# A fused attention and gated-MLP block: second pair of rows turned by products, value rows of the first block ahead of the second block, sums, scales and splits one product apart, first maxima in twos

## The chip, the cores and the metric

One core of one Trainium2 chip runs the whole program. The metric is device time in microseconds, smaller is better; the time given for a kernel is the median of its runs. A profile is one further execution, recorded by the hardware profiler. Engines: PE is TensorE (matrix products), DVE is VectorE, ACT is ScalarE, POOL is GpSimd, SP is SyncE, which here only issues DMAs. PEld is PE's loading of weights.

## The reference

The input `x` has 2048 rows of 576 numbers. A layer norm, an attention of 32 heads of 18 numbers each, a second layer norm and a gated MLP of width 4608 follow, each half with its residual:

```python
qkv = (x @ wqkv).reshape(B, S, 3, H, Dh)            # x: layer norm of A_x
scores = jnp.einsum("bhqd,bhkd->bhqk", q, k) * Dh ** -0.5
p = _softmax(scores, axis=-1)
o = jnp.einsum("bhqk,bhkd->bhqd", p, v)
h = x + o @ wo
...
g = jnp.einsum("bsd,df->bsf", x, w_gate)            # x: layer norm of h
u = jnp.einsum("bsd,df->bsf", x, w_up)
h2 = h + jnp.einsum("bsf,fd->bsd", _gelu(g) * u, w_down)
```

Only the first part matters here: layer norm, the product with `wqkv`, and the start of the attention.

## The kernel before

**Numbers in two halves.** A float32 operand is cut into a rounded float16 part ("high") and the float16 of what is left ("low"). A product of two such operands is three float16 products, high by high, low by high and high by low. Weights are multiplied by a power of two before they are cut: `norm_w` sums their squares on ACT (five passes, L155), adds them over the partitions with one small product on PE (L158) and makes the scale from the result in seven short DVE steps. `split_cols` then makes the high part on ACT (L283) and the low part on DVE (L284). `cut(s, j)` does so for the 128 columns of query and key tile `j`; the value weights (`wf[2]`) are cut in two halves of 288 columns, and land in the memory that `wf[0]` leaves.

**Rows.** The 2048 rows are 16 row tiles of 128, four to a block; there are four blocks. For a row tile, `row_stats` takes mean and variance on DVE (L188, L189), `rstd_of` the reciprocal root for a group of row tiles (root on ACT, the rest on DVE), `normed` the normalized row in place (DVE, L236), `split_rows` the high part on ACT (L248) and the low part on POOL or DVE (L249, L250), and `turn` the transposed row tile, by a transposing DMA (L253) into `XT`, which holds all rows with the 576 features on the partitions. Features 0 to 511 are chunks 0 to 3 (high) and 5 to 8 (low); chunk 4 holds the last 64, high and low. `rstd_beside` is `rstd_of` done by 12 short POOL steps; before, only a later part of the program used it.

**Products of this stage.** `qk_tile(j, b)` makes 128 columns of queries or keys for the 512 rows of block `b`: 14 products of 512 columns (L300) in one of four PSUM banks (`m_ring` over `singles`), then the high part by ACT (L352), the low part by DVE (L353), and two DMAs to DRAM (L355, L356). `v_rows(t)` makes the values of a row tile: twice 14 products of 288 columns in one of two pairs of banks, evicted by ACT (L368, L370). A generator yields after half of the products and after the rest; `take(it, n)` runs `n` such steps.

**Order.** PE, ACT, DVE and POOL run each in the order in which the code is written (`in_order`). So does SP inside its own `manual_schedule`, which before ended with `v_rows(3)`; behind it the framework places SP's DMAs. The order written is: rows 0 and 1 (norm, split, turn), 9 idle products, rows 2 and 3 with 18 idle products (`idle_products`: products that nothing reads), query and key tiles of block 0 with the cutting of their weights and the norms of rows 4 to 11 between them, first tiles of block 1, `v_rows(0)` to `v_rows(3)`, and the other tiles 0, 4 and 5 of blocks 1 to 3.

**Start of the attention.** `init_set(sets[0])` writes constant rows by four DMAs and `load_stacks(0)` loads queries and keys of four heads back from DRAM, one pair of heads by 12 DMAs of SP and one by 12 of POOL. The softmax needs a maximum for each row; `maxima()` makes each from a product (L589) in a bank of `m_ring` and a DVE reduction of 0.68 us (L601). Its steps make 2, 1, 2, 1 and 2 products, in this order. Before the attention's own loop, 60 such steps (L1183) run in turns with 72 steps of `other_products()` (the other values and tiles, "fill"), after 14 steps of fill alone.

Of the kernel before, what the change touches and what calls it, by code (L numbers as in the profile page):

```python
# [18 lines left out]
P = 128  # L19
D = 576  # L20
# [3 lines left out]
NK = 4  # L24
# [7 lines left out]
def tile_block(  # L32
# [202 lines left out]
    def normed(dst, src, t):  # L235
        nc.vector.tensor_scalar(dst, src, rs[:, t : t + 1], nb[:, t : t + 1],  # L236
                                op0=ALU.mult, op1=ALU.add)
# [9 lines left out]
    def split_rows(dst, src, copy=nc.scalar.copy, sub=nc.vector.tensor_sub):  # L247
        copy(dst[:, :D], src)  # L248
        sub(dst[:, LM:], src[:, : NK * P], dst[:, : NK * P])  # L249
        sub(dst[:, D:LM], src[:, NK * P :], dst[:, NK * P : D])  # L250

    def turn(rows, t):
        nc.sync.dma_start_transpose(XT[:, :, t * P : (t + 1) * P], rows)  # L253
# [3 lines left out]
    def load_w(dst, src, eng):  # L257
        eng.dma_start(dst[:, :NK, :], src[: NK * P, :].rearrange("(c p) n -> p c n", p=P))
# [22 lines left out]
    def split_cols(wf, sc, wh, wl):  # L281

        nc.scalar.activation(wh, wf, AF.Copy, scale=sc)  # L283
        nc.vector.scalar_tensor_tensor(wl, wf, sc, wh, op0=ALU.mult, op1=ALU.subtract)  # L284
# [17 lines left out]
    def run(it):  # L302
        for _ in it:
            pass

    def result(it):
        while True:
            try:
                next(it)
            except StopIteration as end:  # L310
                return end.value

    def take(it, n=1):
        for _ in range(n):
            next(it, None)
# [27 lines left out]
    def load_x(b):  # L343
        nc.sync.dma_start(nat[:, b * TPB : (b + 1) * TPB], xv[:, b * TPB : (b + 1) * TPB])

    def qk_tile(j, b, bank):
        sl = slice(b * TB, (b + 1) * TB)
        hl = next(tmp3_ring).bitcast(F16).rearrange("p (a b) -> p a b", a=2)
        hi, lo = hl[:, 0], hl[:, 1]
        yield from accumulate(bank[:, :TB], [(w, a) for a, w in products(  # L350
            sl, *wqk[j], slice(0, P))])
        nc.scalar.activation(hi, bank[:, :TB], AF.Copy, scale=2.0 ** -16)  # L352
        nc.vector.scalar_tensor_tensor(lo, bank[:, :TB], 2.0 ** -16, hi,  # L353
                                       op0=ALU.mult, op1=ALU.subtract)
        nc.sync.dma_start(qk_hi[j * P : (j + 1) * P, sl], hi)  # L355
        nc.sync.dma_start(qk_lo[j * P : (j + 1) * P, sl], lo)  # L356
        yield
# [19 lines left out]
    def norm_w(i):  # L377

        e = yield from norm_exponent(wf[i], f"w{i}")
        e_w.append(e)  # L380
        return pow2(e, -1, 268, f"s_w{i}")

    def cut(s, *js):

        for j in js:
            for i in range(2):
                a, b = max(j * P, i * D), min((j + 1) * P, (i + 1) * D)
                if a < b and s[i] is not None:
                    h, l = (w[:, :, a - j * P : b - j * P] for w in wqk[j])
                    split_cols(wf[i][:, :, a - i * D : b - i * D], s[i], h, l)  # L390
# [3 lines left out]
    def ln_stats(t0, n):  # L394
        for t in range(t0, t0 + n):
            row_stats(nat[:, t], t)

    def ln_rows(t0, n, **engines):
        for t in range(t0, t0 + n):
            normed(nat[:, t], nat[:, t], t)  # L400
        for t in range(t0, t0 + n):
# [19 lines left out]
    def idle_products(n):  # L421

        for _ in range(n):
            nc.tensor.matmul(pairs2[0][:, 0], id16, parts[0][:, :512], start=True, stop=True)

    with tc.manual_schedule(engines={EngineType.SP}):
        n0, n1, n2 = norm_w(0), norm_w(1), norm_w(2)
        s = [None, None]
        ln_stats(0, 2)
        rstd_of(0, 2, root=True)  # L430
        ln_rows(0, 2, **on_pool)
        load_chunks(wf[1], wqkv[:, D:QK], nc.sync, (0, 1))
        idle_products(9)
        ln_stats(2, 2)
        take(n0, 2)
        rstd_of(2, 2, root=True)
        for t in (2, 3):
            normed(nat[:, t], nat[:, t], t)
        take(n0, 3)
        split_rows(parts[2], nat[:, 2], **on_pool)  # L440
        s[0] = result(n0)
# [5 lines left out]
        load_chunks(wf[1], wqkv[:, D:QK], nc.sync, range(2, NK + 1))  # L447
        load_x(1)
        qk_tiles(0, 0)
        take(n1, 4)  # L450
        qk_tiles(0, 1)
        load_x(2)
        take(n1, 1)
        it = qk_tile(2, 0, next(m_ring))
        next(it)
        s = [None, result(n1)]
        cut(s, 4)
        run(it)
        cut(s, 5)
        ln_stats(4, 2)  # L460
        qk_tiles(0, 3)
        cut(s, 6, 7, 8)
        ln_stats(6, 2)
        rstd_of(4, 4, root=True)
        qk_tiles(0, 4)
        ln_rows(4, 2, **on_pool)
        load_w(wf[2], wqkv[:, QK:], nc.sync)
        qk_tiles(0, 5)
        ln_rows(6, 2, **on_pool)
        ln_stats(8, 2)  # L470
        qk_tiles(0, 6)
        load_x(3)
        ln_stats(10, 2)
        rstd_of(8, 4, root=True)
        take(n2, 3)
        qk_tiles(0, 7)
        take(n2, 2)
        ln_rows(8, 2, **on_pool)
        qk_tiles(0, 8)
        ln_rows(10, 2, **on_pool)  # L480
        it = qk_tile(0, 1, next(m_ring))
        next(it)
        s_v = result(n2)
        run(it)
        split_cols(wf[2][:, :, :HALF], s_v, *wv[0])
        ln_stats(12, 2)
        qk_tiles(1, 4)
        split_cols(wf[2][:, :, HALF:], s_v, *wv[1])
        ln_stats(14, 2)
        rstd_of(12, 4, root=True)  # L490
        qk_tiles(1, 5)
        ln_rows(12, 2, **on_pool)
        run(v_rows(0))
        run(v_rows(1))
        ln_rows(14, 2, **on_pool)
        run(v_rows(2))
        run(v_rows(3))
    qk_tiles(2, 0, 4, 5)
    qk_tiles(3, 0, 4, 5)
    nc.vector.tensor_add(e_w[0], e_w[0], e_w[1])  # L500
# [842 lines left out]
```

## Time and profile before

| | us |
|---|---|
| median of 3 runs | 2673.91 (2672.24 to 2674.68) |
| profiled execution, time | 2668.08 |
| profiled execution, span | 2666.3 |
| PE busy | 2589.7 (97%) |
| DVE busy | 2013.1 (76%) |
| ACT busy | 1619.2 (61%) |
| POOL busy | 777.3 (29%) |

A timeline gives for each merged piece its start, its length, the engine, the line, the operation with output and inputs, the count, and in brackets the idle time of the engine ahead of it and what ended that. A windows view gives busy time (and instructions) of each engine in a stretch, the clock granted to PE, the DMA engines' busy share and GB/s. A groups view gives busy time and mean ns of one instruction. The profiled execution was 5.8 us shorter than the median of the runs; differences are worked out inside it and then taken from the median.

### The profile page before, as it was taken

Reading aid. Unit: us, or ns where it says so; the run is one execution under the profiler, and the core shown is the slowest. Engines: PE = TensorE matmul, PEld = TensorE weight load, DVE = VectorE, ACT = ScalarE, POOL = GpSimd, SP = SyncE. Lnnn points to the kernel's source line nnn. Section 1 sums busy time; section 2 is a strip of 40 time slices with the busy share of each in tenths; the row PEclk is TensorE's granted clock in tenths of the full one; section 3 lists DMA queues with packets and bytes.
Section 4 is the critical chain, followed back from the end, with each engine's and each line's share of the span. In section 5 each row is a group of like instructions: output and inputs, shape, how many; then the busy total and the mean of one; then the engine's idle time right before and its main releaser. Section 6 shows DMA issues by size and latency. Waiting matters only on the chain.

```text
span 2666.3 us, 44517 instructions
## 1 busy us (share of the span) xinstructions
PE 2589.7 (97%) x16665; PEld 1118.6 (42%) x16665; DVE 2013.1 (76%) x3872; ACT 1619.2 (61%) x2128; POOL 777.3 (29%) x1040
## 2 busy tenths in 40 slices
PE   6999999999999999999999899999999999999999
PEld 2542222222222222222243555555555555555555
DVE  6367999999999999999967866566666666666653
ACT  5215999999999999999956433333333333333332
POOL 2200352132223232221666532222222222222221
PEclk9999999999999999999999999999999999999999
DMA  8411101010101010110116321010101010101010
GB/s 222 94 40 51 54 26 30 19 42 15 42 14 45 17 42 19 30 25 20 36 47 125 74 51 40 23 40 23 40 22 40 24 39 25 38 27 36 29 59 36
DMA packets 171466, 114.70 MB, mean 43 GB/s; under 512 B 90872, under 2 KB 149772, under 8 KB 171250
## 3 DMA queue, kind: packets, MB, share of 16 engines
q1 hardware_dynamic: 163566, 99.06, 13.9%
q0 software_dynamic: 7552, 12.79, 1.8%
q8 instruction: 130, 2.13, 0.3%
q14 instruction: 86, 0.70, 0.1%
q10 hardware_dynamic: 132, 0.01, 0.0%
HBM read 76.51 MB, written 15.01 MB: 34 GB/s over the span
## 4 chain that ended last, share of the span: by engine, by line
PE 67%; ACT 15%; issue 7%; DVE 4%; POOL 2%; DMA 2%; SPq 0%; ACTq 0%; DVEq 0%; POOLq 0%
PE more L1065 14%; PE bank L1065 13%; ACT WK L644 10%; PE bank L300 10%; PE bank L648 9%; PE more L300 8%; PE bank L589 7%; PE pair L300 4%; ACT nat L595 4%; PE pair L642 2%; DVE mx L601 1%; DMA nat<-rc 1%; ACT nat L662 0%; POOL A L996 0%; DMA V<-V 0%
## 5 line engine op out<-in xcount | busy, mean ns | idle before, releaser
L644 ACT ACTIVATE WK<-pair 128x1024 f32<-128x1024 f32 x1024 | 1000.0, 1041 | 84.8 <-PE pair L642 84.1
L601 DVE TENSOR_REDUCE mx<-bank 128x1 f32<-128x512 f32 x1552 | 975.7, 683 | 42.8 <-PE bank L589 32.4
L648 PE MATMUL bank<-WK,V 128*32 128x512 f32 x4096 | 547.7, 606 | 0.2 <-ACT nat L662 0.2
L300 PEld LDWEIGHTS <-WK 128*128 128x128 f16 x3456 | 338.0, 98 | 90.9 <-ACT WK L1076 1.7
L1065 PEld LDWEIGHTS <-W 128*128 128x128 f16 x2394 | 234.3, 98 | 282.9 <-issue 5.7
L589 PE MATMUL bank<-W 54*128 54x512 f16 x896 | 258.2, 379 | 14.0 <-DVE mx L601 1.8
L589 PE MATMUL bank<-A 54*128 54x512 f16 x904 | 255.0, 380 | 16.8 <-DVE mx L601 5.3
L671 POOL TENSOR_TENSOR rp<-rc,minus_one 128x16 f32<-128x16 f32 x28 | 81.9, 2926 | 537.1 <-DMA rc<-nat 537.1
L300 PE MATMUL more<-W,WK 128*128 128x288 f16 x1728 | 235.6, 286 | 2.2 <-ACT WK L1076 1.4
L300 PE MATMUL bank<-W,WK 128*128 128x288 f16 x1728 | 235.2, 286 | 0.0
L1065 PE MATMUL bank<-X,W 128*128 128x512 f16 x792 | 223.8, 379 | 0.0
L642 PE MATMUL pair<-A 56*128 56x512 f16 x1024 | 212.9, 381 | 2.3 <-ACT WK L644 1.4
L642 PE MATMUL pair<-W 56*128 56x512 f16 x1024 | 210.3, 380 | 4.3 <-ACT WK L644 3.2
L1065 PE MATMUL bank<-V,W 128*128 128x512 f16 x720 | 202.4, 379 | 0.4 <-ACT tmp L1115 0.3
L936 POOL TENSOR_TENSOR A<-A 128x384 f32<-128x384 f32 x136 | 137.0, 1028 | 202.6 <-DMA A<-in_B_w_up_dram 118.7
L589 PEld LDWEIGHTS <-W 54*128 54x128 f16 x1024 | 75.1, 93 | 283.6 <-issue 266.6
L599 DVE CUSTOM_DVE_ANT_0 nat<-bank,nat 128x512 f32<-128x512 f32 x248 | 171.4, 691 | 27.1 <-PE pair L642 4.4
L589 PEld LDWEIGHTS <-A 54*128 54x128 f16 x1024 | 72.3, 93 | 267.9 <-issue 250.8
L1079 POOL TENSOR_TENSOR WK<-tmp,WK 128x512 f16<-128x512 f32 x73 | 87.9, 1203 | 305.9 <-ACT WK L1076 305.6
L1083 ACT COPY tmp<-more 128x512 f32<-128x512 f32 x36 | 21.0, 583 | 236.8 <-PE more L1065 198.2
L595 ACT ACTIVATE nat<-bank 128x512 f32<-128x512 f32 x248 | 151.4, 611 | 11.5 <-PE bank L589 11.5
L648 PEld LDWEIGHTS bank<-WK,V 128*32 128x32 f32 x4096 | 81.1, 108 | 179.0 <-issue 164.2
(304 smaller groups left out, 3259.9 us busy)
## 6 DMA issues: line engine op xcount, KB each, us to landing
A<-in_B_w_down_dram SPq DMA_DIRECT2D x8, 1152.0 KB
nat<-rc SPq DMA_DIRECT2D x32, 256.0 KB
A<-in_B_w_gate_dram SPq DMA_DIRECT2D x64, 128.0 KB
A<-in_B_w_up_dram SPq DMA_DIRECT2D x64, 128.0 KB
qk_hi<-tmp SPq DMA_DIRECT2D x36, 128.0 KB
qk_lo<-tmp SPq DMA_DIRECT2D x36, 128.0 KB
out_dram<-nat SPq DMA_DIRECT2D x16, 288.0 KB
X<-nat SPq DMA_DIRECT2D x100, 36.0 KB
```

The source lines that it names most:

```text
L300: nc.tensor.matmul(dst, a, b, start=(i == 0), stop=(i == len(pairs) - 1))
L589: nc.tensor.matmul(pm[:, :TB], Q[r, q0 : q0 + P], keys, start=True, stop=True)
L595: nc.scalar.activation(row, pm[:, :TB], AF.Relu)
L599: nc.vector.tensor_tensor_reduce(row, pm[:, :TB], row, 1.0, LOWEST, ALU.add, ALU.max, dst)
L601: nc.vector.tensor_reduce(dst, pm[:, :TB], axis=AX.X, op=ALU.max)
L642: nc.tensor.matmul(pS[:, j, :TB], K[r, kt * P : (kt + 1) * P], Q[r, qc * TB : (qc + 1) * TB], start=True, stop=True)
L644: nc.scalar.activation(pes[(2 * kt + pr) % NPE], pS[:, :, :TB], AF.Exp, scale=ex_reg)
L648: nc.tensor.matmul(acc[32 * hh : 32 * hh + 32, :TB], Vg[n // NB][:, kt * G4 + hh * VC : kt * G4 + hh * VC + 32], pes[(2 * kt + hh // 2) % ...
L671: nc.gpsimd.tensor_tensor(rc, den, minus_one.to_broadcast([P, R]), op=ALU.pow)
L936: op(W8[:, d], W8[:, a], W8[:, b])
L1065: nc.tensor.matmul(bank, w, x_, start=start and i == 0, stop=i == len(mm) - 1, skip_group_check=not start)
L1079: nc.gpsimd.tensor_sub(hl[:, 2 * i + j], v, hh[:, 2 * i + j])
```

## The change

`ln_rows` is cut in two, `ln_norm` and `ln_split`. Row tiles 2 and 3 are no longer turned by DMA: the new `turned` multiplies their chunks by a unit matrix on PE (18 products of 128 columns in five banks) and copies the results to `XT` by three ACT and two DVE instructions; the idle products ahead of it go from 18 to 4. The value weights are loaded behind tile 0 of block 0, ahead of the rows of block 2, and cut during tiles 6 and 7; `v_rows(0)` to `v_rows(3)` stand ahead of all tiles of block 1. Rows 4 to 15 take their scales from POOL (`rstd_beside`), and statistics, scales, norms and splits are spread, one or two between two tiles. SP's own written order goes on until `key_steps(0)` (DMAs of the constant rows, the stacks, the keys' steps). The 60 steps of maxima are taken two at a time (30 turns) with 2 or 3 of fill, in place of 2 or 3 at a time (24 turns) with 3.

```diff
+    def turned(t0):
+
+        cols = slice(t0 * P, (t0 + 2) * P)
+        pts = [pairs2[0][:, 1], pairs2[1][:, 0], next(m_ring), next(m_ring)]
+        for pt, c0 in zip(pts, (0, 2, NK + 1, NK + 3)):
+            for c in range(2):
+                for t in range(2):
+                    o = (2 * c + t) * P
+                    nc.tensor.matmul(pt[:, o : o + P], parts[t0 + t][:, (c0 + c) * P : (c0 + c + 1) * P],
+                                     id16, start=True, stop=True)
+            copy = nc.scalar.copy if c0 < NK else nc.vector.tensor_copy
+            copy(XT[:, c0 : c0 + 2, cols], pt.rearrange("p (c t) -> p c t", c=2))
...
-        idle_products(18)
-        split_rows(parts[3], nat[:, 3])
-        turn(parts[2], 2)
-        turn(parts[3], 3)
-        cut(s, 0, 1, 2, 3, 4)
+    idle_products(4)
+    split_rows(parts[3], nat[:, 3])
+    cut(s, 0)
+    turned(2)
+    cut(s, 1, 2, 3, 4)
     load_chunks(wf[1], wqkv[:, D:QK], nc.sync, range(2, NK + 1))
     load_x(1)
     qk_tiles(0, 0)
+    load_w(wf[2], wqkv[:, QK:], nc.sync)
...
+    take(n2, 2)
+    qk_tiles(0, 4)
+    load_x(2)
+    cut(s, 7)
+    ln_stats(6, 1)
+    take(n2, 3)
+    qk_tiles(0, 5)
+    cut(s, 8)
+    ln_stats(7, 1)
+    rstd_beside(4, 4, 1024.0)
+    it = qk_tile(6, 0, next(m_ring))
+    next(it)
+    s_v = result(n2)
+    run(it)
+    ln_norm(4, 2)
+    split_cols(wf[2][:, :, :HALF], s_v, *wv[0])
+    qk_tiles(0, 7)
+    load_x(3)
+    ln_split(4, 1, **on_pool)
+    split_cols(wf[2][:, :, HALF:], s_v, *wv[1])
+    ln_split(5, 1, **on_pool)
+    ln_norm(6, 2)
+    qk_tiles(0, 8)
+    ln_split(6, 2, **on_pool)
+    ln_stats(8, 3)
+    run(v_rows(0))
+    ln_stats(11, 1)
+    rstd_beside(8, 4, 1024.0)
+    ln_norm(8, 2)
+    run(v_rows(1))
+    ln_split(8, 2, **on_pool)
+    ln_norm(10, 2)
+    ln_stats(12, 2)
+    run(v_rows(2))
+    ln_split(10, 2, **on_pool)
+    ln_stats(14, 2)
+    rstd_beside(12, 4, 1024.0)
+    run(v_rows(3))
+    ln_norm(12, 2)
+    qk_tiles(1, 0)
...
     key_steps(0)
+    sp_order.close()
...
-    for i in range(AHEAD):
-        take(mxs, 2 + i % 2)
-        take(fill, 3)
+    for i in range(5 * AHEAD // 4):
+        take(mxs, 2)
+        take(fill, 2 + (i % 5 in (1, 3)))
```

Three places show how the rows stand on an engine. DVE from the low part of row 3 (L249, L250) to the first eviction, first before and then in the change (`bank`, `pair`: PSUM; `W`: cut weights; `X`: the turned rows):

```order
L249 TENSOR_TENSOR A<-nat,A 128x512
L250 TENSOR_TENSOR A<-nat,A 128x64
L284 SCALAR_TENSOR_TENSOR W<-WK,p_s_w_206,W 128x640 x4
L284 SCALAR_TENSOR_TENSOR W<-WK,p_s_w_206,W 128x5x64
L353 SCALAR_TENSOR_TENSOR tmp_81<-bank_67,tmp_81 128x512
```

```order
L249 TENSOR_TENSOR A<-nat,A 128x512
L250 TENSOR_TENSOR A<-nat,A 128x64
L284 SCALAR_TENSOR_TENSOR W<-WK,p_s_w_206,W 128x640
L439 CAST X<-bank_67 128x2x256
L439 CAST X<-bank_68 128x2x256
L284 SCALAR_TENSOR_TENSOR W<-WK,p_s_w_206,W 128x640 x3
L284 SCALAR_TENSOR_TENSOR W<-WK,p_s_w_206,W 128x5x64
L353 SCALAR_TENSOR_TENSOR tmp_81<-bank_66,tmp_81 128x512
```

Two copies of turned low parts now stand between the low weights of tile 0 and those of tiles 1 to 4.

ACT from the second half of the value weights (L283, 128x1440) to the first evictions of values (L368, L370), before and in the change:

```order
L283 ACTIVATE W<-WK,p_s_w_556 128x1440
L199 ACTIVATE ln_r<-mv,eps 128x4
L352 ACTIVATE tmp_81<-bank_68 128x512
L248 CAST A<-nat 128x576 x2
L368 ACTIVATE V<-pair_73 128x4x4x18
L368 ACTIVATE V<-pair_74 128x3x4x18
```

```order
L283 ACTIVATE W<-WK,p_s_w_447 128x1440
L248 CAST A<-nat 128x576
L352 ACTIVATE tmp_81<-bank_68 128x512
L248 CAST A<-nat 128x576 x2
L368 ACTIVATE V<-pair_73 128x4x4x18
L368 ACTIVATE V<-pair_74 128x3x4x18
L370 ACTIVATE V<-pair_74 128x4x18
L368 ACTIVATE V<-pair_73 128x4x4x18
L368 ACTIVATE V<-pair_74 128x3x4x18
L370 ACTIVATE V<-pair_74 128x4x18
L248 CAST A<-nat 128x576 x2
L368 ACTIVATE V<-pair_73 128x4x4x18
```

The root on ACT (L199) is gone; the high parts of rows 6 and 7 now stand ahead of the evictions of `v_rows(0)`, and those of rows 8 and 9 ahead of the evictions of `v_rows(2)`.

SP around the last stores of this stage (L355, L356), the constant rows (`neg`) and the stacks of the first heads, before and in the change:

```order
L355 DMA qk_hi<-tmp_81 128x512
L356 DMA qk_lo<-tmp_81 128x512
L540 DMA A<-qk_hi 18x2048
L355 DMA qk_hi<-tmp_81 128x512
L356 DMA qk_lo<-tmp_81 128x512
L540 DMA A<-qk_hi 18x2048
L355 DMA qk_hi<-tmp_81 128x512
L541 DMA A<-qk_hi 18x2048
L356 DMA qk_lo<-tmp_81 128x512
```

```order
L355 DMA qk_hi<-tmp_81 128x512
L356 DMA qk_lo<-tmp_81 128x512
L556 DMA A<-neg 2x8x256 x4
L572 DMA A<-qk_hi 18x2048
L573 DMA A<-qk_hi 18x2048
L572 DMA A<-qk_hi 18x2048
L573 DMA A<-qk_lo 18x2048
```

Before, three stack loads were issued ahead of the last store and the constant rows long before; now all four and all twelve stand behind it.

More of the change, by code (lines that the diff above doesn't have):

```diff
@@ L424, in idle_products @@
             nc.tensor.matmul(pairs2[0][:, 0], id16, parts[0][:, :512], start=True, stop=True)
[L426 to L441, printed above, removed]
-        idle_products(18)
-        split_rows(parts[3], nat[:, 3])
-        turn(parts[2], 2)
-        turn(parts[3], 3)
-        cut(s, 0, 1, 2, 3, 4)
[L447 to L497, printed above, removed]
@@ new lines, in turned @@
+    def turned(t0):
[9 more added lines that the diff above has]
+            copy(XT[:, c0 : c0 + 2, cols], pt.rearrange("p (c t) -> p c t", c=2))
+        pt = next(m_ring)
+        for t in range(2):
+            nc.tensor.matmul(pt[:, t * P : (t + 1) * P], parts[t0 + t][:, NK * P : (NK + 1) * P],
+                             id16, start=True, stop=True)
+        nc.scalar.copy(XT[:, NK, cols], pt[:, : 2 * P])
@@ new lines, in tile_block @@
+    sp_order = ExitStack()
+    sp_order.enter_context(tc.manual_schedule(engines={EngineType.SP}))
+    n0, n1, n2 = norm_w(0), norm_w(1), norm_w(2)
+    s = [None, None]
+    ln_stats(0, 2)
+    rstd_of(0, 2, root=True)
+    ln_norm(0, 2)
+    ln_split(0, 2, **on_pool)
+    load_chunks(wf[1], wqkv[:, D:QK], nc.sync, (0, 1))
+    idle_products(9)
+    ln_stats(2, 2)
+    take(n0, 2)
+    rstd_of(2, 2, root=True)
+    ln_norm(2, 2)
+    take(n0, 3)
+    split_rows(parts[2], nat[:, 2], **on_pool)
@@ new lines, in tile_block @@
+    s[0] = result(n0)
+    idle_products(4)
[3 more added lines that the diff above has]
+    cut(s, 1, 2, 3, 4)
+    load_chunks(wf[1], wqkv[:, D:QK], nc.sync, range(2, NK + 1))
+    load_x(1)
+    qk_tiles(0, 0)
+    load_w(wf[2], wqkv[:, QK:], nc.sync)
+    take(n1, 4)
+    qk_tiles(0, 1)
+    take(n1, 1)
+    it = qk_tile(2, 0, next(m_ring))
+    next(it)
+    s = [None, result(n1)]
+    cut(s, 4)
+    run(it)
+    cut(s, 5)
+    ln_stats(4, 1)
+    qk_tiles(0, 3)
+    cut(s, 6)
@@ L498, in tile_block @@
+    ln_split(14, 2, **on_pool)
+    qk_tiles(1, 5)
     qk_tiles(2, 0, 4, 5)
```

9 lines of the change are left out of this document (8 added, 1 removed).

## Prediction

> **What bounds the kernel now.** First the busy time by stage (start, length, then busy us and instructions of PE, PEld, DVE, ACT, POOL; granted clock; DMA share; GB/s): up to the first maxima, the maxima beside fill, the rest.
>
> ```profile
> 0.00:118.60 118.60, 92.43 (x495) 49.80 (x495) 58.22 (x154) 48.26 (x104) 32.27 (x64) 0.96 0.68 174
> 118.60:230.60 112.00, 106.51 (x588) 50.01 (x588) 68.69 (x114) 20.45 (x49) 3.84 (x9) 1.00 0.16 51
> 230.60:2666.30 2435.70, 2390.72 (x15584) 1018.77 (x15583) 1886.21 (x3604) 1550.47 (x1976) 741.21 (x967) 1.00 0.14 36
> ```
>
> PE is the bound; all that the change can reach is its idle time in the first two stages, 26.2 and 5.5 us. Behind 230.6 the same rows follow on each engine, so that part should only shift. PE's timeline shows where it stands still:
>
> ```profile
> 13.29 4.04 PE L424 MATMUL pair<-A,id 128*128 128x512 f16 x18
> 20.41 7.71 PE L300 MATMUL bank<-X,W 128*128 128x512 f16 x35 [3.08 <-DMA X<-A]
> 28.33 19.80 PE L300 MATMUL bank<-X,W 128*128 128x512 f16 x91
> 57.41 3.05 PE L300 MATMUL bank<-X,W 128*128 128x512 f16 x7 [9.28 <-DMA X<-A]
> 76.45 12.12 PE L300 MATMUL pair<-W,X 128*128 128x288 f16 x84 [4.32 <-ACT V L368]
> 88.41 18.29 PE L300 MATMUL bank<-X,W 128*128 128x512 f16 x84
> 106.54 12.17 PE L300 MATMUL pair<-W,X 128*128 128x288 f16 x98
> 124.27 0.37 PE L589 MATMUL bank<-A 54*128 54x512 f16 x1 [0.35 <-DVE mx L601]
> ```
>
> The first useful product starts at 20.41 and waits for a turned row; 9.28 us go to the turned rows of block 1, 4.32 us to an eviction of values. The clock falls in the two long gaps but not after the 3.08 us: the 35 products from 20.41 take 0.22 each.
>
> ```profile
> 56.00:60.00 4.00, 2.60 (x7) 0.95 (x8) 2.10 (x4) 3.53 (x9) 1.46 (x3) 0.50 0.96 201
> 76.00:80.00 4.00, 3.55 (x19) 2.40 (x19) 1.08 (x1) 1.18 (x5) 2.62 (x4) 0.66 0.41 76
> ```
>
> In the second stage nearly all idle time is one wait, 14 times, the longest at the start (us, times, longest):
>
> ```profile
> PE bank L589 <- DVE mx L601: 5.5, 14, 0.9
> ```
>
> **Term 1, first tile.** A tile of 14 products takes 3.02 us at full clock (84 in 88.41 to 106.54, 0.216 each), `v_rows` 3.46 (28 at 0.1235, from the 98 at 106.54).
>
> ```profile
> 10.14 2.85 SPq L253 DMA_TRANSPOSE X<-A  x2
> 15.55 2.77 SPq L253 DMA_TRANSPOSE X<-A  x2
> 14.79 3.44 ACT L283 ACTIVATE W<-WK,p_s_w 128x640 f16<-128x640 f32 x5 [0.66 <-DVE p_s_w L173]
> 14.75 0.77 POOL L250 TENSOR_TENSOR A<-nat,A 128x64 f16<-128x64 f32 x1
> 15.28 0.33 DVE L250 TENSOR_TENSOR A<-nat,A 128x64 f16<-128x64 f32 x1
> ```
>
> ```profile
> L188 DVE BATCH_NORM_STATS2 st<-nat 128x6 f32<-128x288 f32 x32 | 12.7, 438 | 2.8 <-DMA nat<-in_A_x_dram 2.8
> L353 DVE SCALAR_TENSOR_TENSOR tmp<-bank,tmp 128x512 f16<-128x512 f32 x18 | 12.3, 684 | 42.0 <-ACT tmp L352 42.0
> L352 ACT ACTIVATE tmp<-bank 128x512 f16<-128x512 f32 x18 | 10.6, 590 | 22.1 <-PE bank L300 19.5 <-issue 2.6
> L236 DVE TENSOR_SCALAR nat<-nat,rs,nb 128x576 f32<-128x576 f32 x16 | 10.6, 707 | 0.1
> L155 ACT ACTIVATE A<-WK 128x576 f16<-128x576 f32 x15 | 10.1, 672 | 3.5 <-DMA WK<-in_A_wqkv_dram 3.4
> L248 ACT CAST A<-nat 128x576 f16<-128x576 f32 x16 | 9.9, 670 | 8.8 <-DVE nat L236 7.1 <-issue 1.7
> L284 DVE SCALAR_TENSOR_TENSOR W<-WK,p_s_w,W 128x640 f16<-128x640 f32 x8 | 6.6, 880 | 0.1
> L284 DVE SCALAR_TENSOR_TENSOR W<-WK,p_s_w,W 128x1440 f16<-128x1440 f32 x2 | 3.4, 1714 | 0.7 <-ACT W L283 0.7
> ```
>
> Rows 2 and 3 are cut by 15.6 as before. A turning product of 128 columns isn't in the trace; it lies between nothing and 0.22 (the 18 unit-matrix products of 512 columns, 4.04 us). I take 0.11, about its weight load (0.1), so 18 end at 16.5. A copy of 512 columns I take like an eviction: 0.59 on ACT, 0.68 on DVE. ACT makes W of tile 0 from 14.8 to 15.6, then the copies to 17.2; DVE the low W to 16.5, then its two copies to 17.8. The second product needs the first DVE copy, so PE runs from 17.2. Rows 0 and 1 still go by DMA, issued 5.4 us ahead of rows 2 and 3 (used at 20.4), so down by about 15. Tile 0 ends at 17.2 + 13 x 0.216 = 20.0, 3.4 us ahead of before (20.41 + 14 x 0.216 = 23.4).
>
> The Trainium skill, "TensorE: Matmul & The Clock Gate", Part 4 on the PE-mode transpose, gives about 275 ns for a 128x128 transpose and says that such work doesn't count as busy for the clock gate. By it the 18 take 5.0 us, and 1.5 us more go if tile 0 then runs at half clock; the sum below would be some 12 instead of 15. The trace speaks against the second half: 3.08 us of nothing cost no clock.
>
> **Term 2, block 0 and its values.** Tiles 0 to 8, two norm products and four `v_rows` end, without other waits, at 20.0 + 8 x 3.02 + 0.9 + 13.8 = 59.0; a norm product took 0.36 (20.41 to 28.33 less 35 x 0.216), and I give the two 0.9, as ACT's squares come later against PE now. The waits come from in-order chains:
>
> ```profile
> 20.00:40.00 20.00, 19.59 (x92) 8.90 (x93) 11.65 (x31) 9.61 (x21) 0.00 (x0) 1.00 0.72 228
> 46.85 0.64 SPq L258 DMA_DIRECT2D WK<-in_A_wqkv_dram  x1
> 53.92 0.68 ACT L155 ACTIVATE A<-WK 128x576 f16<-128x576 f32 x1 [3.42 <-DMA WK<-in_A_wqkv_dram]
> 50.12 5.08 SPq L253 DMA_TRANSPOSE X<-A  x2
> ```
>
> From 13.0 on (the first turning DMAs are out) the DMAs must bring key weights, block 1, value weights (1.33 + 1.18 + 1.33 MB) and take three tiles' stores (0.8 MB): at 228 GB/s they are done at 33.3; bounds are 29 (issue near 22 plus the 7.1 us of 46.85 to 53.92) and 38. ACT, which squares them (L155) between the evictions, then delays the second norm product by 0.9.
>
> ```profile
> 1395.21 0.23 POOL L225 TENSOR_SCALAR ln_v<-mv 128x2 f32<-128x2 f32 x1 [1.43 <-DVE mv L189]
> 1398.81 0.24 POOL L233 TENSOR_SCALAR nb<-ln_u 128x2 f32<-128x2 f32 x1
> 1405.66 0.31 POOL L225 TENSOR_SCALAR ln_v<-mv 128x2 f32<-128x2 f32 x1
> 1411.93 0.23 POOL L233 TENSOR_SCALAR nb<-ln_u 128x2 f32<-128x2 f32 x1
> ```
>
> The scales on POOL take 3.8 us where DVE lets POOL alone and 6.5 at the other place. I take 4.1: DVE waits for them here and has little else. The squares end at 38.1, so tile 5 is evicted at 38.7 and 39.4, the low weights of tile 8 end at 40.3, the statistics of row 7 at 41.3, the scales at 45.4, the norms of rows 4 and 5 at 46.5, the low value weights at 48.2 and 50.6 (an eviction between), the norms of 6 and 7 at 51.7. PE wants the first low value weights at 46.3: it waits 1.9, then 0.7 for the second half. The eviction of `v_rows(0)` stands behind the casts of rows 6 and 7 (52.4): 0.7. Statistics of rows 8 to 11 end at 56.5, scales at 60.6, the casts of 8 and 9 at 62.4, the eviction behind them at 62.8; PE has wanted that bank since 59.7: 3.1. Values so end at 59.0 + 0.9 + 6.4 = 66.3. Rows 6 and 7 are turned by then: before, the last turned row was down 10.5 us after the load ahead of it (46.85 to 57.41), and that load, block 3, goes out near 49.7, which gives 60.2. That is the cover of the 9.28 us; each microsecond past 66.3 would cost one. The 4.32 us and the slow clock (1.5 us on the 7 products of 57.41, 1.6 on the 84 of 76.45) go too, as no gap passes 3.1 by this sum. Nine tiles end at 66.3 + 27.2 = 93.5, before at 106.5: **13.0 less**.
>
> **Term 3, stacks.**
>
> ```profile
> 71.76 0.86 SPq L524 DMA_DIRECT2D A<-neg  x1
> 108.15 0.33 SPq L356 DMA_DIRECT2D qk_lo<-tmp  x1
> 113.32 0.28 SPq L541 DMA_DIRECT2D A<-qk_hi  x1
> 119.87 0.12 PEld L589 LDWEIGHTS <-A 54*128 54x128 f16 x2 [1.14 <-DMA A<-qk_lo]
> ```
>
> Before, the last of SP's stacks went out 5.2 us behind the last store and was down 6.6 later; PE waited 0.9. Now four constant rows (0.7 to 0.9 each, 2.9) and three more stacks (1.1) lie between: with the store at 94.9 the last goes out at 104.1. Down 6.6 later, it holds PE from 105.9 to 110.7, 3.9 more than before; down 2.1 later (as the turned rows, issued by 18.3, used at 20.4) it costs nothing and the old 0.9 goes. POOL's half still runs beside, but starts earlier: I take **3.0 more**.
>
> **Term 4, maxima in twos.** Turns of 3, 3, 4, 3 and 3 products fit four banks; before, every second turn made 5 and the fifth waited for a reduction.
>
> ```profile
> L601 DVE TENSOR_REDUCE mx<-bank 128x1 f32<-128x512 f32 x1552 | 975.7, 683 | 42.8 <-PE bank L589 32.4
> ```
>
> Three reductions take 2.05 us, a turn with two steps of value fill 0.6 + 1.73: no wait, though thinly; beside tiles (3.02) amply. Of the 5.5 us all but the first 0.9 go: **4.6 less** (bounds 0 and 5.5). Turns and fill are the same in number, so nothing is added.
>
> **Sum.** 13.0 - 3.0 + 4.6 = 14.6. The profiled execution would take 2668.1 - 14.6 = 2653.5; the median, 5.8 above it, 2673.9 - 14.6 = 2659.3.
>
> **Rivals.**
> - *POOL's scales take the longer row.* 2.4 us more, twice, in the chain to the values; the wait of 3.1 becomes 5.5, longer than the 4.32 that lost the clock, so 1.6 more: 2673.9 - 8.2 = 2665.7. For it: both rows are the same twelve steps, and 64 columns of low part took POOL 0.77 at 14.75 beside DVE's 0.33. Against: DVE waits for most of that time. The Trainium skill, "GPSIMD Engine Reference", section 8, says POOL shares its SBUF interfaces with VectorE and contends where that has two SBUF inputs; the longer row would fit, the trace doesn't name its cause. Chance 0.14.
> - *Everything is covered:* no wait among the values (7.3) and none for the stacks: 13.0 + 7.3 + 4.6 + 0.9 = 25.8, 2648. Against it stands the same chain in the 4.32 us of before. 0.10.
> - *The value weights land at 38,* not 33.3: 4.7 us more ahead of the second norm product, 2664. 0.10.
> - *The twos don't do what they say,* since DVE is late for another reason: 4.6 lost, 2663.9. 0.06.
> - *Slower: turned rows of block 1 late.* In SP's order rows 6 and 7 stand behind tile 8's low store, which waits for DVE, and behind block 3's load, with four more turning DMAs next. From 66.3 on each microsecond costs one; the gain is gone when row 7 lands at 80.9, and beyond 86 the kernel is slower by more than 0.2%. A landing at 88 gives 2673.9 + 7.1 + 1.5 (clock) = 2682. For it: the 9.28 us were this very wait. Against: 60.2 by the old rows. 0.05.
>
> **How the numbers follow.** The forecast, 2659, has 0.55. 0.2%, 5.3 us, is about what a measurement of this kernel can tell from no change. Faster by more than that are the forecast but for its edge, and the first four rivals: 0.89; within it 0.07; slower 0.04. The range goes from part of the covered case, 2650, to past the slow scales, 2668; it leaves out the rest of the covered case and the slower one.
>
> **What would show it.** In PE's timeline: first product of a tile near 17 (term 1 wrong if near 20 or at 0.43 a product); value products from about 45 to 66 with waits named L284 and L368; no wait on turned rows; a wait of 3 to 5 us at the first maxima that names the stacks; and no 0.35 us waits behind it. The prediction is wrong if the first maxima start later than about 113, or if PE's busy time behind them grows.

## The result, and the profile after

| | before | after |
|---|---|---|
| median, us | 2672.69 (2667.78 to 2674.68, 6 runs) | 2654.24 (2649.01 to 2655.46, 6 runs) |
| ratio | | 0.9932, 95% interval 0.9922 to 0.9942 |
| profiled execution, time, us | 2668.08 | 2654.51 |
| span, us | 2666.3 | 2652.7 |

The kernel is faster by 18.4 us, with an interval of 15.5 to 20.8 (the ratio's, times 2672.69). The two profiled executions lie only 13.6 us apart; that gap is taken up below. The stages of after, cut at the same three places as before (start, length, then busy us and instructions of PE, PEld, DVE, ACT, POOL; granted clock; DMA share; GB/s):

```profile
0.00:105.30 105.30, 89.93 (x499) 49.12 (x499) 57.43 (x138) 48.91 (x104) 43.67 (x100) 0.98 0.72 188
105.30:217.20 111.90, 105.30 (x587) 49.80 (x588) 68.20 (x114) 22.07 (x51) 3.83 (x9) 0.97 0.17 53
217.20:2652.70 2435.50, 2389.83 (x15583) 1019.44 (x15582) 1886.77 (x3605) 1550.06 (x1974) 740.68 (x967) 1.00 0.14 36
```

The third stage is 2435.50 us long, as before 2435.70: all of the gain lies in front. Over the first two stages PE's idle time fell from 31.7 to 22.0 us, and its busy time by 3.7; 14 idle products fewer account for 3.1 of that at 0.22 each, the 18 turning products add some 1.5, and the rest was not followed up. PE's timeline of after (start, length, engine, line, operation, count, and in brackets the wait ahead):

```profile
13.70 0.64 PE L436 MATMUL pair<-id,A 128*128 128x128 f16 x8
16.75 7.50 PE L300 MATMUL bank<-X,W 128*128 128x512 f16 x34 [0.67 <-DVE X L439]
45.69 1.88 PE L300 MATMUL pair<-W,X 128*128 128x288 f16 x14 [1.06 <-DVE W L284]
48.22 1.63 PE L300 MATMUL pair<-W,X 128*128 128x288 f16 x12 [0.66 <-DVE W L284]
51.06 7.02 PE L300 MATMUL pair<-W,X 128*128 128x288 f16 x56 [1.21 <-ACT V L368]
60.89 5.07 PE L300 MATMUL pair<-W,X 128*128 128x288 f16 x28 [2.81 <-ACT V L368]
65.80 27.36 PE L300 MATMUL bank<-X,W 128*128 128x512 f16 x126
93.00 12.29 PE L300 MATMUL pair<-W,X 128*128 128x288 f16 x98
107.46 0.37 PE L621 MATMUL bank<-A 54*128 54x512 f16 x1 [2.17 <-DMA A<-qk_hi]
111.01 1.01 PE L621 MATMUL bank<-A 54*128 54x512 f16 x2 [3.18 <-DMA nat<-qk_hi]
```

The 9.28 us for turned rows are gone: the nine tiles of block 1 run in one piece from 65.80. The last of them ends at 93.00, 13.5 us earlier than before (106.54). Four waits of 0.7 to 2.8 us stand among the values, named L284 and L368. Two waits, 5.35 us together, stand at the first maxima, where before there was one of 0.9. And the clock is not full everywhere: 28 values take 5.07 us, which took 3.46 by the prediction's row. The windows view shows it in the column behind the five engines (1.00 is the full clock):

```profile
57.12:60.53 3.41, 0.96 (x8) 0.63 (x7) 1.85 (x4) 1.24 (x3) 1.59 (x7) 1.00 0.65 126
60.53:63.94 3.41, 3.05 (x13) 1.87 (x13) 3.34 (x9) 1.81 (x6) 3.41 (x5) 0.50 0.32 60
112.00:116.00 4.00, 4.00 (x20) 2.14 (x20) 1.18 (x3) 0.47 (x2) 1.46 (x3) 0.61 0.10 23
```

The granted clock was 0.50 for 3.41 us from 60.53 on, where the wait of 2.81 us ends, and 0.61 in the mean of the 4 us behind the wait of 3.18 us.

### The profile page after: what moved, and what is told of

The parts are those of the page before. It is cut to its first block, busy times and chain, and to the rows that moved or that the text cites. A ratio compares the mean times of both kernels' runs of the same rounds, so it can differ in the third digit from the quotient of the medians.

```text
span 2652.7 us, 44543 instructions
## 1 busy us (share of the span) xinstructions
PE 2585.1 (97%) x16669; PEld 1118.4 (42%) x16669; DVE 2012.4 (76%) x3856; ACT 1621.0 (61%) x2128; POOL 788.2 (30%) x1076
## 4 chain that ended last, share of the span: by engine, by line
PE 68%; ACT 16%; issue 8%; DVE 4%; DMA 2%; POOL 2%; SPq 1%; ACTq 0%; DVEq 0%; POOLq 0%
PE more L1097 14%; PE bank L1097 14%; PE bank L300 11%; ACT WK L676 11%; PE bank L680 9%; PE more L300 8%; PE bank L621 7%; ACT nat L627 4%; PE pair L300 4%; PE pair L674 2%; DVE mx L633 1%; DMA nat<-rc 1%; DVE st L188 0%; DMA V<-V 0%; ACT nat L694 0%
```

## The experiments

Ten other kernels were run, and before and after once more. Each is compared with the kernel before on the same chip (2672.6 to 2673.4 in the three groups of runs), so that ratios may be set beside each other. "Against after" below is the difference of medians from 2654.24; a difference of 4 us between two changed kernels is about as much as their intervals can separate, so gains of 3.6 to 4.6 us over after stand on the waits in the traces as much as on the medians.

### Each part undone or done alone

**Rows 2 and 3 turned by DMAs again.**

```diff
-    idle_products(4)
+    idle_products(18)
     split_rows(parts[3], nat[:, 3])
+    turn(parts[2], 2)
+    turn(parts[3], 3)
     cut(s, 0)
-    turned(2)
```

> The changed kernel with row tiles 2 and 3 turned by DMA again (and 18 idle products), all else as changed. Theory: the first product of tile 0 starts at 20 instead of 16.8 and all behind it moves by about 3.5 us, less what the waits among the values give back. Rival (the values' chain on DVE and POOL, not the first product, sets their end): the first product is 3.5 us later, but the last tile of this stage ends less than 1.5 us later.

Measured: 2662.84 us, ratio 0.9958 (0.9945 to 0.9972), 8.6 us slower than after. PE's timeline of this kernel at the first tile:

```profile
20.02 10.54 PE L300 MATMUL bank<-X,W 128*128 128x512 f16 x35 [3.30 <-DMA X<-A]
```

The start moves back by 3.3 us (16.75 to 20.02), as forecast. The clock takes 2.8 more: the 35 products took 10.54 us where before's profile had 7.71 behind a wait of 3.08 us. Both together make nearly all of the 6.3 us by which the first scores start later than in after (223.53, 217.22). The rest of this profile's loss, 3.4 us, lies behind the first scores, where the clock was at half for 10.2 us, in after for 3.4; that part was not looked into. So the turning by products is worth its 3.3 us and, in executions that lose the clock here, some 3 more.

**Values behind the second block's first tiles.** The four `v_rows` stand behind `qk_tiles(1, 5)` instead of among block 0's splits.

```diff
-    run(v_rows(0))
...
-    run(v_rows(3))
...
     qk_tiles(1, 5)
+    run(v_rows(0))
+    run(v_rows(1))
+    run(v_rows(2))
+    run(v_rows(3))
```

> The changed kernel with the four value rows of block 0 moved behind the first three tiles of block 1, where they stood before. Theory (the value rows cover the turning of block 1): PE waits for turned rows at the first tile of block 1, from about 44 to 58 or 60, some 14 us, then at half clock for 1.5 us, while the waits among the values (5.7 us) go; the last tile ends about 10 us later than in the changed kernel. Rival (the turned rows are ready early and the gain came from the earlier loads): a wait of under 5 us and no loss.

Measured: 2662.45 us, ratio 0.9962 (0.9949 to 0.9975), 8.2 us slower than after. PE's timeline where block 1 begins:

```profile
58.86 11.24 PE L300 MATMUL bank<-X,W 128*128 128x512 f16 x42 [14.26 <-DMA X<-A]
```

Without the values in front PE stands for 14.26 us, waiting for a turned row, and block 1 cannot start before 58.86. In after it starts at 65.80, and the last of these turning DMAs leaves SP 0.9 us later than here (57.69, 56.78), so by estimate some 6 us of slack were left to the turned rows. This shows that the wait for them is what the values cover.

**Maxima in the old turns,** in after, **and in twos alone,** in before.

```diff
-    for i in range(5 * AHEAD // 4):
-        take(mxs, 2)
-        take(fill, 2 + (i % 5 in (1, 3)))
+    for i in range(AHEAD):
+        take(mxs, 2 + i % 2)
+        take(fill, 3)
```

> The changed kernel with the old turns (2 or 3 steps of maxima, then always 3 of fill). Theory (a turn of five products in four banks waits for a reduction): the waits of 0.35 us come back, 12 or 13 of them, and the stage from the first maxima to the first scores is 4 to 5 us longer than in the changed kernel. Rival (the four microseconds came from the shorter pieces of fill or from the clock): the waits come back and the stage is longer by less than 2 us.

> The kernel before with one edit of the change alone, the first maxima in twos. Theory: of the 14 waits of 5.5 us only the first (0.9, for the stacks) stays; the stage from the first maxima to the first scores falls from 112 to about 107.5 us and the kernel gains 4.5 us. Rival (the gain needs the rest of the change): less than 2 us.

Measured: the old turns 2660.89, ratio 0.9953 (0.9939 to 0.9966), 6.6 us slower than after; the twos alone 2667.31 over 11 runs, ratio 0.9979 (0.9970 to 0.9988), 6.0 us faster than before over 22. The waits view of PE from the second product of the maxima to the first scores (us in total, times, longest), first for the old turns, then for after:

```profile
PE bank L621 <- DVE mx L633: 4.2, 12, 0.4
```

```profile
PE bank L621 <- DVE mx L631: 1.3, 1, 1.3
```

With the old turns the second product of the maxima starts at 110.41 and the first scores at 222.87, 112.5 us; in after it is 111.01 to 217.22, 106.2. That is 6.3 us, though the waits of the turns are 4.2 and after has a new one of 1.3, just ahead of the scores. A wait of 0.35 costs more than itself. Before's timeline, one turn of five and one of three, then after's with a turn of four:

```profile
123.10 0.82 PE L589 MATMUL bank<-A 54*128 54x512 f16 x4
124.58 2.75 PE L300 MATMUL pair<-W,X 128*128 128x288 f16 x21
127.25 0.61 PE L589 MATMUL bank<-A 54*128 54x512 f16 x3
127.79 2.75 PE L300 MATMUL pair<-W,X 128*128 128x288 f16 x21
```

```profile
118.53 0.61 PE L621 MATMUL bank<-A 54*128 54x512 f16 x4
119.07 1.89 PE L300 MATMUL pair<-W,X 128*128 128x288 f16 x14
```

Three products take 0.54 us to the next fill (127.25 to 127.79), and four take no longer (118.53 to 119.07): the two products of one step run side by side, as the starts show (in before two at 187.98). The turn of five, steps of 2, 1 and 2, took 1.48. Without a wait it would take about 0.75, by an estimate of one place more than the turn of three (0.82 less 0.61, the busy times). So the turn is 0.7 too long, not 0.35: the product that was held starts late and also loses its place beside its partner. Twelve turns of five and twelve of three are 24.2 us, thirty turns of three or four 16.2; with the 1.3 us that after waits ahead of the scores, 6.7 us of gain are left, near the 6.3 measured.

### The stacks

**SP's written order ends one step earlier,** so that the constant rows and the stacks may go out between the tiles' stores.

```diff
     mxs = maxima()
+    sp_order.close()
     init_set(sets[0])
     load_stacks(0)
     load_ends(0)
     key_steps(0)
-    sp_order.close()
```

> SP's written order ends ahead of the constant rows, so that they and the first stacks stand among the last stores again, as before. Theory (the order of SP's queue holds the first maxima): the two waits at the first maxima, 2.2 and 3.2 us in the changed kernel, shrink to about 1 us together as before, and the half clock on the fill behind them goes: 4 to 6 us faster than the changed kernel. Rival (the stacks are held by the DMA engines, 24 loads at a time): the waits stay at 3 us or more in all and at most 2 us are won. All of it is computed.

Measured: 2649.59 us, ratio 0.9915 (0.9901 to 0.9928), 4.6 us faster than after. SP's queue (issue of DMAs), first in after, then in this kernel:

```profile
94.54 0.32 SPq L356 DMA_DIRECT2D qk_lo<-tmp  x1
94.95 2.90 SPq L556 DMA_DIRECT2D A<-neg  x4
...
106.19 0.26 SPq L573 DMA_DIRECT2D A<-qk_hi  x1
```

```profile
84.04 0.67 SPq L556 DMA_DIRECT2D A<-neg  x1
...
95.56 0.34 SPq L356 DMA_DIRECT2D qk_lo<-tmp  x1
...
100.27 0.29 SPq L573 DMA_DIRECT2D A<-qk_hi  x1
```

In after four constant rows and all of SP's stacks stand behind the last store, and the last stack leaves 11.65 us behind it; here it leaves 4.7 us behind. PE's timeline of this kernel then has one wait left of the two:

```profile
106.33 0.39 PE L621 MATMUL bank<-A 54*128 54x512 f16 x1
109.30 0.59 PE L621 MATMUL bank<-A 54*128 54x512 f16 x2 [2.58 <-DMA nat<-qk_hi]
```

The wait of 2.17 at the first product is gone and the other is 0.6 shorter. The half clock on the fill behind it, which was to go too, stayed: 14 products took 3.54 us from 109.82 on. From the end of the last tile to the second product pass 15.3 us here (93.96 to 109.30), 18.0 in after and 13.4 in before, so the profiles show 2.7 us of the 4.6. More than half of the loss that the prediction named is the place of one statement.

### The scales on POOL

**The scales of rows 8 to 11 on DVE,** in after.

```diff
-    rstd_beside(8, 4, 1024.0)
+    rstd_of(8, 4)
```

> The changed kernel with the scales of rows 8 to 11 on DVE (13 short steps, about 2.5 us) instead of POOL (4.2 us). Theory (the wait of 2.8 us ahead of the last value rows is the chain statistics, scales, norm, cast, eviction): that wait falls by about 1.7 us to about 1, and the end of the stage moves by the same. Rival (the eviction waits for ACT or for the statistics): the wait stays within 0.5 us of 2.8.

Measured: 2650.63 us, ratio 0.9919 (0.9906 to 0.9933), 3.6 us faster than after. In after POOL starts the twelve steps at 54.43 and is done 4.2 us later; DVE's timeline ahead of the norms (L236), in after and then here:

```profile
58.67 2.89 DVE L236 TENSOR_SCALAR nat<-nat,rs,nb 128x576 f32<-128x576 f32 x4 [4.33 <-POOL nb L233]
```

```profile
56.77 2.89 DVE L236 TENSOR_SCALAR nat<-nat,rs,nb 128x576 f32<-128x576 f32 x4
```

and PE's last values here:

```profile
59.03 3.59 PE L300 MATMUL pair<-W,X 128*128 128x288 f16 x28 [1.14 <-ACT V L368]
```

DVE does in 2.5 us (54.19 to 56.73) what it waited 4.33 us for. The wait of 2.81 us becomes 1.14, and behind it the clock is full: 3.59 us for what took 5.07 (and 3.59 in after's second profile, below). The chain of the prediction, from POOL's scales over norms and casts to the eviction, is the one that ends last here.

### The clock behind waits of about 3 us

Waits of almost one length lost the clock in one profile and kept it in another: 28 values behind 2.80 us took 3.59 us with the old turns, and 5.07 behind 2.81 in after. Three kernels fill such waits with idle products, whose results are read by nothing. What decides it is worked out in the last section.

**Idle products in before,** 12 more at the first tile, 40 and 18 in its two later waits, **and in after,** 10 ahead of the last values, 9 and 13 at the first maxima:

```diff
+    def warm(n):
+        for _ in range(n):
+            nc.tensor.matmul(pairs2[0][:, 1], id16, XT[:, 0, :512], start=True, stop=True)
...
+    warm(10)
     run(v_rows(3))
```

> The kernel before with products that nothing reads in its three long waits: 30 instead of 18 ahead of the first tile, 40 ahead of the first tile of block 1, 18 ahead of the second value row. The waits stay. Theory (besides its waits the kernel before lost clock behind each, 1.5 and 1.6 us in the profile and in most executions some 2.9 more behind the 3.1 us wait, which that profile escaped): 4 to 6 us faster than before. Rival (the clock loss behind the first wait is rare): about 3 us faster.

> The changed kernel with products that nothing reads in three of PE's waits: 10 ahead of the last value row, 9 ahead of the first maximum and 13 ahead of the second (2.2, 1.9 and 2.8 us at full clock), so that PE is idle less than a microsecond there. Theory (a wait of 2.8 to 3.3 us costs the clock in some executions, as the 28 value products behind it took 5.07 us in one profile and 3.59 in another): those products and the fill behind the first maxima run at full clock, the median falls by 2 to 3 us. Rival (the clock falls for another reason, or the products hold up what comes behind): within 1 us of the changed kernel.

Measured: before with them 2677.66, ratio 1.0018 (1.0009 to 1.0028); after with them 2654.41, ratio 0.9930 (0.9917 to 0.9944). No gain in either, for a reason of the experiment. PE's timeline at the values of the second:

```profile
60.73 3.82 PE L431 MATMUL pair<-X,id 128*128 128x512 f16 x10 [2.81 <-ACT V L368]
64.39 3.59 PE L300 MATMUL pair<-W,X 128*128 128x288 f16 x28
```

The idle products wrote into a bank of the pair whose eviction the values wait for, so they waited for the same eviction and then stood in front: 3.7 us given, 1.5 gained. In before 18 of them did the same at 77.87 and took 6.30 us, and 30 at the first tile ran past the wait that they were to fill. Neither says what the clock costs.

**The same in after, with the ten written to a free bank:**

```diff
+    warm(10, singles[3])
     run(v_rows(3))
```

> The kernel after with ten idle products in the wait ahead of the last values, written to a bank that waits for nothing there, and nine and thirteen in the two waits of the first maxima. No needed product starts later for them if they end with the wait. Theory (slow clock behind the waits costs 1.5 us at the values and 1.7 us at the fill in most executions): about 2.5 us quicker than after, 2651 to 2652, a ratio near 0.992, the 28 values in 3.6 us and the 14 fill products in 1.7. Rival (the loss is rare, or the idle products overrun the waits): no change against after, 2654, or 1 us slower.

Measured: 2650.51 us (2647.71 to 2650.95), ratio 0.9914 (0.9900 to 0.9927), 3.7 us faster than after, which had 2649.01 to 2655.46.

```profile
58.77 2.32 PE L431 MATMUL bank<-X,id 128*128 128x512 f16 x10
61.76 3.59 PE L300 MATMUL pair<-W,X 128*128 128x288 f16 x28 [0.67 <-ACT V L368]
...
110.45 0.60 PE L632 MATMUL bank<-A 54*128 54x512 f16 x2
110.98 1.89 PE L300 MATMUL pair<-W,X 128*128 128x288 f16 x14
```

All of it runs at full clock: 3.59 us for the 28 values, 1.89 for the 14 fill products, 3.43 in after. The wait itself stays as long; only the clock behind it is kept. By the medians the lost clock costs after 3.7 us, at the edge of what they can separate; in its two profiles it cost 3.0 us (both places) and 1.7 (the fill alone).

### A second profile of each kernel

Before and after were run again, unchanged.

> The kernel before, unchanged, profiled a second time. Between the two profiles the change moved the first scores 13.6 us forward, between the medians 18.5 us. Theory (the first profile of before was one of its quicker executions): here the 35 products behind the wait of about 3.1 us for the turned rows take 9 to 10.5 us instead of 7.71, or the first maxima wait 3 to 5 us for the stacks instead of 0.9, as they did in the kernel with the twos alone (9.24 and 4.87), and the first scores start 2 to 5 us later than 230.81. Rival (the profile of before is typical, the gap is elsewhere): 7.7 and 0.9 again, first scores at 230.8 within 0.5, and the difference sits in the 2435.5 us behind.

> The kernel after, unchanged, profiled a second time. Theory (the clock behind waits of 2.8 to 3.3 us is lost in some executions only): the values behind the wait of 2.8 us take 3.6 or 5.1 us, the fill behind the wait of 3.2 us 1.7 or 3.4 us, and first scores lie between 213.9 and 217.3. Rival (the loss is fixed by the length of the wait): 5.1 and 3.4 again, first scores at 217.2 within 0.3.

Measured: before 2672.82, after 2652.12. Where the stages end in the four profiles (start of a row in PE's timeline, us):

| | before, 1st | before, 2nd | after, 1st | after, 2nd |
|---|---|---|---|---|
| last tile ends | 106.54 | 107.28 | 93.00 | 92.05 |
| second product of the maxima | 119.90 | 122.26 | 111.01 | 109.07 |
| first scores | 230.81 | 234.80 | 217.22 | 215.58 |
| from there to the end | 2435.5 | 2436.2 | 2435.5 | 2434.7 |

PE's timeline of the second profile of before at the first tile and the maxima, and of the second of after at the last values:

```profile
13.22 5.71 PE L424 MATMUL pair<-A,id 128*128 128x512 f16 x18
20.12 7.71 PE L300 MATMUL bank<-X,W 128*128 128x512 f16 x35 [1.19 <-DMA X<-A]
...
122.26 0.87 PE L589 MATMUL bank<-A 54*128 54x512 f16 x2 [2.25 <-DMA nat<-qk_lo]
123.07 4.09 PE L300 MATMUL pair<-W,X 128*128 128x288 f16 x21
```

```profile
60.84 3.59 PE L300 MATMUL pair<-W,X 128*128 128x288 f16 x28 [2.80 <-ACT V L368]
```

This before waits 2.25 us for the stacks where the first waited 0.9, and loses the clock behind it (4.09 us for 21 products, 2.75 in the first). The first tile, where the theory had looked for most of it, was no slower: there the 18 idle products ran more slowly (5.71 us, 4.04 in the first profile), but inside the wait. This after kept its clock at the values (3.59, not 5.07) and lost it at the fill again. Taken as means of two, the last tile ends 14.4 us earlier, the step to the second maximum is 3.3 longer, the maxima are 5.4 shorter, and the part behind is 0.7 shorter: 17.2 in sum, against 18.4 by the medians. The first pair of profiles had one of before's quickest executions (2668.08; the lowest of its nine runs beside these two was 2669.14) and one of after near its median.

### The two gains together

Both edits that helped, in after: SP's order ended one step earlier, and the scales of rows 8 to 11 on DVE.

> The kernel after with the statement that ends SP's written order ahead of the constant rows and stacks, and with the scales of rows 8 to 11 on DVE. Theory (the two costs lie at different places, one in the wait for the stacks and one in the wait of the last values): the two gains add, 4.6 and 3.6 us, so 2646, a ratio of 0.990; last values wait about 1.1 us at full clock and the first maxima 2.6 us at one place. Rival (values that end earlier only wait longer for the stacks): the gain of the first alone, 2649.6, with 4 to 6 us of waits at the first maxima.

Measured: 2647.58 us (2645.02 to 2648.37, 4 runs), ratio 0.9903 (0.9887 to 0.9918), 6.7 us faster than after and the fastest kernel of all; its interval lies below that of after.

```profile
59.95 3.59 PE L300 MATMUL pair<-W,X 128*128 128x288 f16 x28 [1.14 <-ACT V L368]
82.55 9.22 PE L300 MATMUL bank<-X,W 128*128 128x512 f16 x42 [0.88 <-DMA X<-A]
105.94 0.59 PE L621 MATMUL bank<-A 54*128 54x512 f16 x2 [1.84 <-DMA nat<-qk_hi]
```

Both waits are short and no clock is lost. Of the 8.2 us that the two brought singly, 6.7 are left; a new wait of 0.88 us for turned rows of a later block has appeared, probably because the tiles now reach them earlier.

## Why the prediction was right

The forecast was 2659 us with a range of 2650 to 2668; the time is 2654.24. The likeliest course is the one that happened, wait for wait but for one of 0.9 us; the clock behind the waits and the size of term 4 were off.

- **Term 1, the first tile.** The second product at 17.2 in the prediction, at 16.75 in the trace; 3.4 us of gain were forecast, and 3.3 measured by the undo. Of the 18 turning products 8 took 0.64 us, and the 34 products behind them ran at 0.22, so nothing was lost here. The price of 275 ns for each transpose and a half clock behind them, by the Trainium skill's page "TensorE: Matmul & The Clock Gate", Part 4, did not come; the page speaks of the transpose mode, and these are plain products by a unit matrix. (By that price, all of it on the path, the prediction's sum would also have been about 10, not 12: 3.0 and 1.5 us less.) What the term left out is the clock that is lost there in part of the executions: the kernel with the twos alone, whose first tile is before's, took 9.24 us for its 35 products behind 3.12 us. The prediction took from one profile that a wait of 3.08 us costs none.
- **Term 2, the values.** Waits of 1.9, 0.7, 0.7 and 3.1 were forecast, and are 1.06, 0.66, 1.21 and 2.81. The 0.9 at the second norm product is not there: ACT's squares of the value weights start at 30.39 with no wait for a DMA, so these had landed ahead of the forecast 33.3, and the rival that had them at 38 fell. POOL's scales took 4.2 us both times (4.1 taken; the rival had 6.5). The values were to end at 66.3, 13.0 us of gain in all; block 1 starts at 65.80 and at 64.27 in the two profiles, and the gain is 13.5, or 14.4 as a mean of two. "No gap passes 3.1 by this sum" was right of the gap, but not that such a gap costs no clock: 1.5 us in the first profile.
- **Turned rows of block 1.** Forecast down at 60.2, covered until 66.3. Without cover they let PE start at 58.86, which makes about 59.8 in after, by the estimate above.
- **Term 3, the stacks.** The last store at 94.54 (94.9 forecast), the last stack out at 106.19 (104.1), the second maximum product at 111.01 (110.7). 3.0 more were taken; the first pair of profiles shows 4.7, the means 3.3. The fill's slow clock behind the wait, about 1.5 us, comes on top and was not in the sum.
- **Term 4, the twos.** 4.6 us were taken, from the waits' own length. Measured are 6.3 by the profile and 6.6 by the medians when undone, 6.0 when done alone. The term counted the wait and left out that the held product loses its place beside its partner: 0.7 a turn, not 0.35. Nor is the number of turns the same, as it said: 24 became 30, of 0.54 us each; and a wait of 1.3 us ahead of the scores came new.
- **Sum.** 14.6 us were forecast, 18.4 measured. With the sizes of the runs, as means of two profiles: 14.4 less 3.3 plus 5.4, and 0.7 behind, is 17.2. The step that missed is that the sum was made against one execution of before, 2668.1, taken as like the others but for a constant 5.8 us. That difference was not constant. In the second profile it was mainly wait and clock at the stacks (2.25 us instead of 0.9, and 1.3 us of clock), at a place that the change touches. Over the 40 runs of before beside the other kernels the time goes with the mean granted clock, from 2666.26 us at 0.997 to 2678.17 at 0.993, with 0.995 as the median; the first profile had 0.996, and after's six runs 0.996 to 0.999.

The rival "all covered", 2648, did not come, but the last kernel above reaches 2647.6 by undoing two costs that the change itself had brought.

## What to carry to other kernels

When work is moved ahead to fill a wait, look at what its in-order queues now hold back: here one statement that pinned SP's order held the stacks behind all stores and cost 4.6 us by the medians (2.7 by the profiles), and one chain of scales on an otherwise idle engine cost 3.6 on the path. A short wait that comes back in every turn can cost more than its length, where the product that is held would have run beside another. Take two profiles before you make a sum against one, above all where PE waits for 2 us or more: up to about 3.9 us (the last section), whether the clock is lost differs from one execution to the next.

## What the runs showed of the hardware

**The clock changes on a grid of 3.41 us, and a wait costs it when enough of it falls between two lines of the grid.** Within each profile all changes of the granted clock lie whole multiples of 3.41 us apart. In after it is 0.50 from 60.53 to 63.94 and again from 108.31 to 115.14, 14 to 16 pieces later. Where the grid lies differs from one execution to the next. After's wait of 2.81 us fell almost whole into the piece from 57.12 to 60.53 (PE busy for 0.96 us, in the view of the result above), and the clock was lost. In after's second profile a line of the grid, at 59.31, cut the wait of 2.80 us in two, and the clock was kept:

```profile
55.90:59.31 3.41, 2.14 (x18) 1.56 (x16) 0.69 (x2) 0.07 (x1) 1.95 (x10) 1.00 1.02 211
59.31:62.72 3.41, 1.88 (x16) 1.50 (x16) 3.38 (x7) 2.97 (x7) 2.73 (x3) 1.00 0.01 2
```

The fourteen profiles were laid on their grids, from the first rise of the clock to the first scores. A fall from the full clock came behind 24 pieces, and in each PE had been idle for 1.94 us or more; no piece with 1.92 or less was followed by one. So the waits sort themselves: 3.08 us were kept, split into 1.92 and 1.15, and 3.30 lost, with 2.21 in one piece. The shortest single wait with a loss was 1.95 us, whole in one piece, with the values behind the second block: the clock fell at 76.62, 1.15 us behind the wait, and 24 products took 4.77 us, 2.96 at 0.1235 each. Behind 1.84 us, in the last kernel, it was kept. By this a lone wait of less than 1.9 us would never cost the clock here, one of more than 3.9 (twice 1.94) always, and what lies between would depend on the grid; this is an estimate from the 24 pieces. In the scores, whose products read fewer rows, the clock fell behind less idle time (0.99 us in after's piece from 217.54), so the 1.94 us hold for the products ahead of them only. The Trainium skill, "TensorE: Matmul & The Clock Gate", Part 1, says that the gate watches a window of about 3.4 us that runs freely; the grid of 3.41 us agrees. The loss behind 1.95 us also says that the window need not be idle as a whole.

**POOL is slow beside DVE's low value weights, and DVE's norms beside POOL.** DVE's timeline of after, at the low value weights (L284, which read two arrays of SBUF) and the norms of rows 6 and 7:

```profile
46.15 2.01 DVE L284 SCALAR_TENSOR_TENSOR W<-WK,p_s_w,W 128x1440 f16<-128x1440 f32 x1
48.09 1.90 DVE L236 TENSOR_SCALAR nat<-nat,rs,nb 128x576 f32<-128x576 f32 x2
```

and POOL's beside it, the low parts of rows 4 and, later, of rows that have DVE's other work beside them:

```profile
44.31 2.35 POOL L249 TENSOR_TENSOR A<-nat,A 128x512 f16<-128x512 f32 x1 [1.40 <-ACT A L248]
46.61 1.72 POOL L250 TENSOR_TENSOR A<-nat,A 128x64 f16<-128x64 f32 x1
50.12 1.16 POOL L249 TENSOR_TENSOR A<-nat,A 128x512 f16<-128x512 f32 x1
51.23 0.31 POOL L250 TENSOR_TENSOR A<-nat,A 128x64 f16<-128x64 f32 x1
```

POOL took 2.35 and 1.72 us for what it does in 1.16 and 0.31 a little later, and in before too 64 columns took 1.79 us at 64.73, beside the same L284. DVE took 1.90 us for two norms, beside POOL's low parts of row 5, that took 1.07 at 42.94 with POOL idle. No run takes the one away to time the other. These norms stand in the chain to the values' first eviction, which may be why PE's wait there was 1.21 us instead of 0.7; it was not tried apart.
